# A written-out order of a two-stage kernel on one core, laid out anew for the landings of its first loads

## The chip, the core and the metric

The kernel runs on one core of a Trainium2 chip. A core has five engines that run side by side, each with its own queue of instructions which it works off in order: TensorE (PE, matmuls; PEld is its weight load), VectorE (DVE), ScalarE (ACT), GpSimd (POOL) and SyncE (SP, which here only issues DMAs). Matmuls write to PSUM, eight banks of 128 x 2 KB; ACT and DVE bring the results from there to the on-chip memory SBUF. The metric is the device time of one launch in microseconds, the median of several runs.

## What is computed

```python
# x (8, 8, 512, 64), state (8, 8, 32, 64): per batch b and head h
scores  = 0.125 * x @ state^T;   a  = softmax(scores over the 32 states)
scores2 = 0.125 * state @ x^T;   a2 = softmax(scores2 over the 512 tokens)
y = concat([a @ state, a2 @ x], axis=2)          # 8 x 8 x 544 x 64
h = y.reshape(8 * 544, 512) @ w_in               # w_in 512 x 2048
g = max(h, 0) + alpha * min(h, 0)                # alpha 2048
out = g @ w_out                                  # w_out 2048 x 512
```

## The kernel before

The kernel never forms `a @ state`: it multiplies the states with w_in first (m = state @ w_in, per batch and per quarter f of w_in's columns, on PE), and then h = a @ m. All operands of matmuls are 16 bit, sums are 32 bit. A batch has 512 tokens and 16 groups of 128 columns of h, called jc.

All work is cut into some fifty kinds of step (each a small function, lines 160 to 608), and the string ORDER (lines 17 to 102) writes out in which order the steps are issued: about 1060 words, each a step's name with its arguments, read at line 625. An engine's queue gets its instructions in that order. What has to wait for what (data, a buffer or a bank that is still read) is turned into semaphores by the framework. So the order decides three things: the place of each instruction in its engine's queue, the engine where a word carries a letter (a = ACT, v = DVE, p = POOL), and the PSUM bank where it carries a bank's number (0 to 5). The banks that are left make one double tile named `two`.

The words, by engine:

- POOL's queue. `lx0`: second half of the first x (L191, 256 KB as stored). `id`: the identity matrix. `lst`: the states of batches 1 to 7 (L207). `wi.f`: a quarter of w_in (L213). `wo.i`: a quarter of w_out (L219). `lx.b`: x of batch b (L162). All are DMA issues, and these loads turn 32 bit into 16. `ssh.p` subtracts the maximum (L360), `snorm.p` multiplies by one over the sum (L374), `tn` the same for the second softmax (L419).
- DMAs ahead of ORDER: the first half of the first x in two pieces (SP and ACT, L179), the states of batch 0 (ACT, L185), alpha (SP, L187).
- PE. `Z.k.n`: n matmuls of zeros into bank k (L232), which compute nothing. `stt`, `str.i.k`: transposed states of batch 0, of the others (L247). `xt.b.j.g.k`: four transposes of x of batch b into bank k (L299). `sc.b` (or `sc.0.0`, `sc.0.1` by halves): scores into `two` (L313). `m.b.f.k0.k1`: the two halves of m into two banks, or into `two` if no banks are given (L463). `f.b.jc.g.k`: half of one jc of h (L517). `F.b.jc.k`: one jc of h, two matmuls (L496). `S.b.q.j.k`: two of the 16 matmuls of an output row block q of batch b, with jc 2j and 2j+1 (L548). `rd.b.k`: the second softmax's reads (L438). `R`, `L`: the last blocks (L596, L568).
- ACT or DVE. `xc`: first x to 16 bit (L197). `sto`, `sro`: transposed states out of PSUM (L261, L281). `xo.b.j.g`: transposed x out (L304). `mo.b.f.e.g`: half g of m out (L485). `O`, `RO`, `LO`: outputs out, then a DMA on SP. `rdo`: the reads out (L449).
- DVE. `stc`: states to 16 bit (L253). `oma`: 1 - alpha (L269, L270). `sb`: scores as blocks (L348, L346). `smax`, `ssum`: maximum, sum and its reciprocal (L354, L370, L371). `wb`: the weights back, called aT (L382). `tm`, `tsum`: the second softmax's maximum and reciprocal (L394, L397, L415). `G.b.jc`: gt, the activation's result (L536).
- ACT. `sexp`, `te`: exponentials (L366, L405). `N.b.jc`: neg = max(-h, 0) (L528), which G reads.
- SP. `xd.b`, `tt.b`: transposes by DMA of x from batch 2 on, and of the second softmax's weights.

The first batch runs its first softmax by halves, so that f.0.jc.0 can start on the first half. m of several batches is made early, as soon as the first quarter of w_in is there. The slots of x hold four batches, those of m seven.

```python
    for token in (globals().get("TOKENS") or ORDER).split():
        name, *args = token.split(".")
        steps[name](*[int(a) if a.isdigit() else a for a in args])
```

Of the kernel before, what the change touches and what calls it, by code (L numbers as in the profile page):

```python
# [29 lines left out]
smax.1 N.0.11 S.0.2.3 m.0.3 G.0.8 F.0.10.5 tn.0.1 S.0.0.3 mo.0.3.a.0 G.0.9 N.0.10 G.0.11 ssh.p.1  # L30
S.0.3.0.3 mo.0.3.v.1 S.0.3.1 F.0.13.0 S.0.3.2 sexp.1 N.0.13 G.0.10 S.0.3.3 m.1.3 ssum.1 G.0.13
F.0.14.5 S.0.2.4 snorm.p.1 N.0.14 G.0.14 S.0.1.4 wb.1 tt.0 F.0.12.0 N.0.12 G.0.12 S.0.0.4 F.0.15.5
S.0.3.4 mo.1.3.a.1 N.0.15 tsum.1 tn.1.0 S.0.1.5 G.0.15 S.0.0.5 S.0.2.5 F.1.0.0 S.0.1.6 mo.1.3.a.0
F.1.2.5 N.1.0 lx.3 S.0.1.7 S.0.2.6 N.1.2 S.0.2.7 sc.2 O.0.2.a G.1.0 O.0.1.v G.1.2 S.0.0.6 S.0.0.7
F.1.5.0 F.1.1.1 F.1.6.5 tm.2 F.1.3.2 O.0.0.a xd.3 N.1.5 sb.2 S.0.3.5 N.1.1 F.1.7.4 G.1.5 S.0.3.6
N.1.6 N.1.3 S.0.3.7 F.1.4.0 G.1.1 S.1.2.0.1 te.2.1 G.1.3 N.1.7 N.1.4 O.0.3.a G.1.7 F.1.14.2 S.1.2.1
te.2.0 F.1.9.4 G.1.6 N.1.14 G.1.4 smax.2 rd.0.3 m.2.3 F.1.11.5 N.1.9 mo.2.3.a.1 G.1.9 F.1.8.0 tn.1.1
rdo.0.a G.1.14 mo.2.3.a.0 tt.1 ssh.p.2 N.1.8 S.1.2.2 lx.4 F.1.10.3 N.1.11 S.1.1.0.4 N.1.10 S.1.2.3
G.1.8 sexp.2 S.1.1.1 m.3.2 G.1.11 m.2.1.2.0 G.1.10 mo.3.2.a.0 S.1.1.2 mo.2.1.a.0 ssum.2 F.1.12.5
N.1.12 S.1.1.3 F.1.13.3 snorm.p.2 S.1.1.4 G.1.12 F.1.15.2 N.1.13 S.1.1.5 S.1.2.4 xd.4 S.1.2.5 N.1.15  # L40
mo.2.1.a.1 G.1.13 mo.3.2.a.1 G.1.15 S.1.1.6 m.2.2.5.3 mo.2.2.a.1 m.3.1.0.2 sc.3 wb.2 sb.3 S.1.2.6
mo.3.1.a.0 mo.2.2.a.0 S.1.2.7 S.1.0.0.3 mo.3.1.a.1 F.2.3.0 O.1.2.a S.1.0.1 N.2.3 smax.3 F.2.12.5
N.2.12 G.2.3 F.2.4.2 N.2.4 G.2.12 F.2.2.1 S.1.1.7 F.2.15.0 S.1.0.2 O.1.1.a tm.3 S.1.3.0.5 F.2.0.4
N.2.15 ssh.p.3 S.1.0.3 G.2.4 S.1.3.1 S.1.0.4 F.2.1.2 S.1.3.2 N.2.2 G.2.2 N.2.0 G.2.15 sexp.3 F.2.9.1
G.2.0 S.1.3.3 tsum.2 F.2.6.0 S.1.0.5 N.2.1 G.2.1 S.1.0.6 F.2.13.4 ssum.3 S.1.3.4 N.2.9 te.3.1
F.2.11.2 te.3.0 S.1.3.5 S.1.3.6 N.2.6 G.2.9 G.2.6 F.2.5.1 N.2.13 S.1.3.7 G.2.13 S.1.0.7 N.2.11
G.2.11 N.2.5 O.1.3.a tn.2.0 O.1.0.a F.2.7.0 rd.1.4 G.2.5 m.4.3.2.5 sc.4 m.3.3.1.3 tsum.3 rdo.1.a
mo.4.3.a.1 snorm.p.3 mo.3.3.a.1 wb.3 tn.2.1 N.2.7 mo.3.3.v.0 S.2.1.0.4 lx.5 mo.4.3.v.0 F.3.4.5 G.2.7
S.2.1.1 F.2.8.3 F.2.10.1 N.3.4 S.2.1.2 N.2.8 G.3.4 tt.2 F.3.6.2 N.2.10 G.2.8 G.2.10 F.3.8.0
S.2.0.0.5 N.3.8 F.3.7.3 N.3.6 S.2.1.3 S.2.1.4 N.3.7 F.3.9.1 S.2.0.1 N.3.9 S.2.1.5 tn.3.0 sb.4 tn.3.1  # L50
G.3.7 G.3.8 G.3.9 F.2.14.3 S.2.0.2 S.2.1.6 F.3.13.0 S.2.0.3 F.3.14.1 smax.4 xd.5 S.2.0.4 G.3.6
N.2.14 S.2.0.5 G.2.14 S.2.3.0.2 S.2.3.1 F.3.2.3 S.2.3.2 N.3.14 S.2.3.3 tm.4 N.3.13 S.2.0.6 ssh.p.4
G.3.14 S.2.3.4 S.2.0.7 F.3.1.1 G.3.13 F.3.3.0 sexp.4 te.4.1 ssum.4 te.4.0 N.3.2 S.2.1.7 S.2.3.5
G.3.2 S.2.3.6 tsum.4 S.2.3.7 tt.3 N.3.1 N.3.3 O.2.1.a O.2.0.a G.3.1 m.6.0 G.3.3 O.2.3.a mo.6.0.a.1
m.5.1.3.1 mo.6.0.v.0 snorm.p.4 m.4.2.4.0 rd.2.5 rd.3.2 mo.4.2.a.0 mo.5.1.a.0 rdo.3.a mo.4.2.v.1
rdo.2.v sc.5 m.4.1.4.0 m.5.0.5.3 mo.5.1.v.1 S.2.2.0.2 mo.4.1.a.0 F.3.10.1 tn.4.1 F.3.5.4 tn.4.0
mo.5.0.a.0 mo.4.1.a.1 N.3.10 tm.5 mo.5.0.a.1 S.2.2.1 F.3.11.5 S.2.2.2 F.3.0.0 S.2.2.3 wb.4 N.3.5
S.2.2.4 N.3.11 G.3.10 N.3.0 F.3.12.3 N.3.12 F.4.0.1 S.2.2.5 sb.5 G.3.5 S.2.2.6 lx.6 S.2.2.7 lx.7
te.5.0 F.4.9.4 N.4.0 te.5.1 G.3.11 G.3.12 G.3.0 tsum.5 O.2.2.a F.3.15.5 F.4.6.3 S.3.3.0.0 S.3.3.1
N.4.9 G.4.0 S.3.3.2 S.3.3.3 S.3.3.4 N.3.15 smax.5 S.3.3.5 F.4.5.2 G.3.15 G.4.9 F.4.3.1 tt.4 N.4.6  # L60
tn.5.0 tn.5.1 N.4.3 S.3.3.6 F.4.1.5 G.4.6 G.4.3 N.4.5 tt.5 S.3.0.0.4 G.4.5 S.3.0.1 F.4.4.3 N.4.4
S.3.0.2 ssh.v.5 N.4.1 F.4.2.1 S.3.3.7 S.3.0.3 S.3.0.4 O.3.3.a sexp.5 S.3.0.5 G.4.4 F.4.7.2 G.4.1
S.3.0.6 N.4.7 S.3.1.0.3 S.3.1.1 ssum.5 S.3.1.2 G.4.7 F.4.8.0 F.4.11.5 N.4.8 S.3.0.7 N.4.2 snorm.v.5
N.4.11 S.3.1.3 xd.6 S.3.1.4 S.3.1.5 O.3.0.a S.3.1.6 G.4.2 rd.4.2 G.4.8 rdo.4.a G.4.11 rd.5.1
m.5.3.4.0 rdo.5.a m.5.2.5.2 sc.6 wb.5 tm.6 mo.5.3.a.0 mo.5.2.a.1 S.3.2.0.1 S.3.2.1 F.4.10.4 N.4.10
S.3.2.2 S.3.2.3 S.4.1.0.2 S.3.1.7 S.4.1.1 S.3.2.4 mo.5.3.a.1 G.4.10 sb.6 smax.6 S.3.2.5 te.6.0
F.4.13.0 O.3.1.v N.4.13 F.5.15.4 N.5.15 G.4.13 S.4.1.2 S.3.2.6 S.3.2.7 te.6.1 F.4.12.3 F.4.14.0
ssh.p.6 m.6.3 G.5.15 mo.5.2.a.0 S.4.1.3 N.4.12 F.5.12.5 S.4.1.4 S.4.1.5 F.5.13.4 N.4.14 O.3.2.v
N.5.12 mo.6.3.v.0 G.4.12 S.4.0.0.1 N.5.13 G.5.12 G.4.14 sexp.6 F.5.3.3 S.4.0.1 F.5.0.5 G.5.13 tsum.6
N.5.3 mo.6.3.v.1 F.4.15.0 S.4.0.2 G.5.3 N.4.15 F.5.1.4 S.4.0.3 tn.6.0 F.5.2.3 S.4.1.6 S.4.0.4 G.4.15  # L70
N.5.0 S.4.1.7 S.4.0.5 xd.7 F.5.5.0 N.5.2 G.5.2 O.4.1.v F.5.10.3 S.4.0.6 N.5.1 G.5.0 N.5.5 N.5.10
G.5.1 m.6.1.2.5 m.7.0 S.4.0.7 S.4.3.0.4 mo.7.0.a.1 O.4.0.a G.5.5 S.4.3.1 mo.6.1.a.0 mo.7.0.v.0
S.4.3.2 G.5.10 F.5.8.0 mo.6.1.a.1 m.6.2.1.2 sc.7 m.7.2.3.5 ssum.6 S.4.3.3 sb.7 S.4.3.4 mo.6.2.a.1
mo.7.2.a.1 N.5.8 snorm.p.6 F.5.4.2 mo.7.2.a.0 S.4.2.0.5 S.4.3.5 S.4.2.1 S.4.2.2 S.4.2.3 smax.7
S.4.3.6 F.5.9.3 N.5.4 wb.6 S.4.3.7 G.5.4 S.4.2.4 mo.6.2.a.0 G.5.8 F.5.7.1 O.4.3.v N.5.9 G.5.9
S.5.2.0.2 ssh.p.7 tn.6.1 F.5.6.0 N.5.7 F.5.14.4 N.5.6 N.5.14 G.5.7 G.5.6 S.4.2.5 F.6.8.3 G.5.14
S.4.2.6 S.5.2.1 S.4.2.7 S.5.2.2 S.5.0.0.1 O.4.2.a sexp.7 S.5.0.1 tm.7 F.5.11.0 N.6.8 tt.6 F.6.3.4
ssum.7 F.6.0.5 G.6.8 S.5.2.3 N.5.11 S.5.0.2 N.6.3 G.5.11 S.5.0.3 G.6.3 te.7.0 snorm.v.7 S.5.0.4
N.6.0 S.5.2.4 te.7.1 F.6.15.3 S.5.1.0.0 S.5.1.1 tsum.7 F.6.1.4 S.5.1.2 N.6.1 G.6.0 G.6.1 N.6.15
S.5.1.3 S.5.1.4 wb.7 F.6.14.5 tn.7.0 S.5.0.5 S.5.1.5 F.6.7.4 G.6.15 S.5.2.5 S.5.2.6 N.6.14 F.6.10.3  # L80
S.5.1.6 S.5.0.6 G.6.14 S.5.2.7 N.6.7 tn.7.1 S.5.0.7 N.6.10 G.6.7 F.6.9.5 G.6.10 O.5.2.v F.6.5.4
N.6.5 O.5.0.v G.6.5 F.6.4.3 tt.7 F.6.6.2 S.5.3.0.1 S.5.3.1 N.6.9 N.6.6 S.5.1.7 S.5.3.2 F.6.2.4 G.6.6
S.5.3.3 S.5.3.4 O.5.1.a N.6.4 m.7.3.2.0 m.7.1 G.6.9 N.6.2 rd.6.5 G.6.4 rd.7.3 mo.7.3.a.1 rdo.7.a
S.5.3.5 F.7.0.0 S.5.3.6 rdo.6.v mo.7.3.v.0 mo.7.1.a.1 F.8.10.5 S.5.3.7 G.6.2 N.7.0 O.5.3.a G.7.0
F.6.13.3 F.6.12.2 N.8.10 S.6.0.0.4 G.8.10 N.6.12 F.6.11.0 S.6.0.1 N.6.13 F.8.3.1 G.6.12 S.6.0.2
N.6.11 F.7.3.5 G.6.11 mo.7.1.v.0 N.8.3 F.8.4.2 G.8.3 S.6.1.0.0 S.6.1.1 N.7.3 S.6.1.2 G.6.13 N.8.4
F.7.7.1 S.6.0.3 F.7.2.3 S.6.1.3 G.8.4 S.6.0.4 N.7.7 F.8.14.2 S.6.0.5 S.6.1.4 S.6.0.6 N.8.14 S.6.0.7
G.7.7 G.8.14 F.8.2.1 S.6.1.5 F.7.6.2 O.6.0.v G.7.3 F.8.9.4 S.6.1.6 S.6.2.0.5 N.8.2 N.7.2 S.6.2.1
# [569 lines left out]
```

## Time and profile before

| what | value |
|---|---|
| median of 3 runs | 218.68 us (218.29 to 218.93) |
| the profiled execution: its time, its span | 219.14 us, 217.3 us |
| PE busy, share of the span | 211.0 us, 97% |
| DVE, ACT, POOL busy | 169.2, 138.0, 64.8 us |
| moved by DMA | 23.39 MB, mean 108 GB/s; 196 GB/s from 1.1 to 25 us |
| issue and landing of the first loads | lx0 1.23 and 6.9; lst 2.74 and 8.3; wi.0 3.32 and 10.9; lx.1 4.07 and 13.6; wi.1 4.94 and 16.2; wo.0 5.83 and 18.7; wi.2 6.57 and 22.1; wo.1 12.35 and 23.9; wi.3 14.64 and 26.5 |

The span runs from the first instruction to the last; the rest of the profiled execution's time lies around it. A busy PE is not a PE at its peak: matmuls overlap, and a matmul of 512 columns is listed with 379 ns while the next one starts 216 ns after it. In a timeline a row is: start, busy time, engine, line, operation, what is written and read, shapes and count, and in brackets the idle time before it with what ended it.

### The profile page before, as it was taken

How to read it: one execution, taken by the hardware profiler on the slowest of the kernel's cores; microseconds unless marked ns; L12 is line 12 of the kernel's file. 1: busy time of each engine (PE TensorE's matmuls, PEld its weight loads, DVE VectorE, ACT ScalarE, POOL GpSimd, SP SyncE). 2: the span in 40 equal slices, each digit the busy share in tenths (PEclk: the TensorE clock that was granted, in tenths of full speed). 3: DMA queues.
4: the chain of work that ended last, by engine and by line, in shares of the span. 5: the costliest groups of instructions: out<-in, count | busy, mean ns of one | idle time of the engine just before them, and what ended most of it. 6: DMA issues, size and time to landing. Idle time of an engine off the chain costs nothing.

```text
span 217.3 us, 4301 instructions
## 1 busy us (share of the span) xinstructions
PE 211.0 (97%) x1692; PEld 104.1 (48%) x1692; DVE 169.2 (78%) x260; ACT 138.0 (63%) x271; POOL 64.8 (30%) x54
## 2 busy tenths in 40 slices
...
GB/s 148 180 205 207 206 202 160 63 250 168 98 162 3 168 109 113 148 129 163 103 142 0 134 62 98 0 108 41 0 195 51 0 48 51 48 38 10 51 97 145
DMA packets 39316, 23.39 MB, mean 108 GB/s; under 512 B 21872, under 2 KB 35328, under 8 KB 39296
## 3 DMA queue, kind: packets, MB, share of 16 engines
...
## 4 chain that ended last, share of the span: by engine, by line
PE 90%; DVE 6%; DMA 1%; ACT 1%; POOL 0%; issue 0%
PE o L548 49%; PE h L496 24%; PE m_ps L463 3%; PE h L505 3%; PE o L596 3%; DVE gt L536 2%; PE sr_ps L438 2%; PE o L568 2%; DMA st<-in_state_dram 1%; PE sc L313 1%; PE z L232 1%; PE xT_ps L299 1%; DVE aT L382 1%; DVE m L485 1%; DVE r L370 1%; DVE nb L394 1%
## 5 line engine op out<-in xcount | busy, mean ns | idle before, releaser
L548 PE MATMUL o<-w_out_sb,gt 128*128 128x512 f16 x496 | 126.4, 379 | 0.1
L528 ACT ACTIVATE neg<-h 128x512 f32<-128x512 f32 (+1 forms) x144 | 77.4, 580 | 45.2 <-PE h L496 31.4
L536 DVE SCALAR_TENSOR_TENSOR gt<-neg,oma_sb,h 128x512 f16<-128x512 f32 x128 | 89.7, 736 | 15.4 <-ACT neg L528 14.6
L548 PEld LDWEIGHTS <-gt 128*128 128x128 f16 x496 | 47.3, 98 | 54.9 <-issue 3.7
L496 PE MATMUL h<-aT,m 128*128 128x512 f16 x250 | 69.2, 379 | 0.3 <-DVE gt L536 0.3
L496 PEld LDWEIGHTS <-m 128*128 128x128 f16 x250 | 24.2, 98 | 29.7 <-issue 1.6
L419 POOL TENSOR_SCALAR e<-e,r 128x512 f16<-128x512 f16 x16 | 25.0, 1568 | 25.2 <-DVE r L415 20.6
L485 ACT CAST m<-m_ps 128x512 f16<-128x512 f32 x50 | 27.9, 603 | 3.7 <-PE m_ps L463 2.0
L360 POOL TENSOR_TENSOR ts<-ts,mx 128x1024 f32<-128x1024 f32 (+1 forms) x8 | 13.6, 1698 | 43.6 <-DVE mx L354 43.6
L586 ACT COPY osb<-o 128x512 f32<-128x512 f32 x22 | 12.8, 591 | 16.4 <-PE o L548 16.4
L374 POOL TENSOR_TENSOR an<-ts,r 128x1024 f16<-128x1024 f32 (+1 forms) x7 | 11.7, 1667 | 18.1 <-DVE r L371 18.0
L405 ACT ACTIVATE e<-sc,nb 128x512 f16<-128x512 f32 x16 | 11.1, 697 | 1.5 <-issue 1.5
L463 PE MATMUL m_ps<-w_in_sb,stT 64*32 64x512 f16 x256 | 11.7, 383 | 0.1
L536 DVE SCALAR_TENSOR_TENSOR gs<-neg,oma_sb,h 128x256 f16<-128x256 f32 x16 | 7.5, 476 | 5.1 <-ACT neg L528 5.1
L370 DVE TENSOR_REDUCE r<-ts 128x32 f32<-128x1024 f32 (+1 forms) x9 | 9.8, 1093 | 1.3 <-ACT ts L366 1.3
L485 DVE CAST m<-m_ps 128x512 f16<-128x512 f32 x14 | 9.3, 684 | 1.6 <-ACT m L485 1.4
L382 DVE STREAM_TRANSPOSE aT<-an 128x1024 f16<-128x1024 f16 (+1 forms) x9 | 10.0, 1114 | 0.5 <-POOL an L374 0.4
L354 DVE TENSOR_REDUCE mx<-ts 128x32 f32<-128x1024 f32 (+1 forms) x9 | 9.9, 1096 | 0.1
L394 DVE TENSOR_REDUCE nb<-sc 128x2 f32<-128x1024 f32 x8 | 9.7, 1212 | 0.1
L232 PE MATMUL z<-zero 128*128 128x128 f16 x76 | 7.6, 263 | 1.9 <-DVE zero L226 1.1
L606 DVE COPY osr<-o 128x512 f32<-128x512 f32 x1 | 0.7, 692 | 11.3 <-PE o L596 11.3
L505 PE MATMUL h<-XS,w_in_sb 128*128 128x256 f16 x64 | 9.4, 273 | 0.0
...
## 6 DMA issues: line engine op xcount, KB each, us to landing
...
w_in_sb<-in_moe_w_in_dram POOLq DMA_DIRECT2D x4, 512.0 KB, 11.6
...
```

The costliest lines, as they stand in the source:

```text
L360: engine(e).tensor_tensor(ts, ts, over_blocks(cols(live["mx", b], j, S // N)), ALU.subtract)
L370: nc.vector.tensor_reduce(r1, blocks(cols(live["ts", b], j, S)), AX.X, ALU.add)
L382: nc.vector.transpose(cols(live["aT", b], j, S), cols(live["an", b], j, S))
L419: nc.gpsimd.tensor_scalar_mul(e2, e2, live["r2", b][:, g : g + 1])
L463: nc.tensor.matmul(t[N * k : N * (k + 1), :], st_head(b, h)[64 * r : 64 * r + 64, :], w_in_sb[64 * r : 64 * r + 64, c, 512 * f : 512 * (f ...
L485: copier(e)(m_tile(b)[:, f, g, :], live["mp", b, f][g])
L496: nc.tensor.matmul(h.rearrange("p (r j s) -> p r j s", r=2, j=2), ms[b][:, f, g, 128 * j : 128 * (j + 1)], weights(b, g), start=(g == 0), ...
L505: nc.tensor.matmul(h, w_in_sb[:, c, 128 * jc : 128 * (jc + 1)], XS[:, c].rearrange("p q n b -> p (q n b)"), start=(c == 0), stop=(c == n_c ...
L528: nc.scalar.activation(neg, h, RELU, bias=0.0, scale=-1.0)
L536: nc.vector.scalar_tensor_tensor(gt, negs.pop((b, jc)), oma_sb[:, jc : jc + 1], h, ALU.mult, ALU.add)
L548: nc.tensor.matmul(outs[b, q], gts[b, jc][:, 128 * q : 128 * (q + 1)], w_out_sb[:, jc, :], start=(jc == 0), stop=(jc == n_jc - 1),)
L586: copier(e)(osb, t)
```

## The change

Only the string ORDER changes, all of it; no function does. The same steps are issued in another order, with other banks, and some on another engine. The part that lies at the start:

```diff
-lx0 id lst stc xc.1.v xc.0.a oma wi.0 lx.1 Z.1.20 stt.0 Z.2.9 xt.0.1.0.1 xt.0.0.0.2 xo.0.1.0.v
-xo.0.0.0.v sto.a Z.0.7 sc.0.0 xt.0.1.1.3 xt.0.0.1.4 str.0.5 sb.0.0 xo.0.0.1.v xo.0.1.1.a Z.1.4
-sc.0.1 smax.0.0 str.1.0 sro.0.a wi.1 sb.0.1 wo.0 smax.0.1 wi.2 ssh.p.0.0 sro.1.a sexp.0.0 Z.1.3 sc.0
-m.0.0.1.2 ssh.p.0.1 mo.0.0.a.0 Z.5.5 m.1.0.3.4 m.2.0.5.0 tm.0 mo.2.0.a.0 ssum.0.0 sexp.0.1
-mo.1.0.a.0 mo.2.0.a.1 wo.1 Z.1.12 m.3.0.1.5 Z.3.7 xt.1.1.0.3 snorm.p.0.0 mo.1.0.v.1 te.0.1
-mo.3.0.a.1 ssum.0.1 wb.0.0 xt.1.0.0.4 xo.1.1.0.v te.0.0 xo.1.0.0.v wi.3 xt.1.1.1.0 snorm.p.0.1 Z.3.9
-f.0.0.0.5 mo.0.0.a.1 xo.1.1.1.v xt.1.0.1.3 wo.2 f.0.2.0.4 tsum.0 m.1.1 wb.0.1 mo.3.0.a.0 xo.1.0.1.v
-m.0.1.0.2 mo.1.1.v.0 tn.0.0 mo.0.1.v.0 f.0.2.1 f.0.0.1 mo.1.1.a.1 mo.0.1.a.1 f.0.1.0.1 f.0.1.1
-F.0.3.3 m.4.0 N.0.0 N.0.1 F.0.5.2 N.0.2 F.0.4.0 G.0.0 G.0.1 N.0.3 G.0.2 F.0.7.5 N.0.5 N.0.4 G.0.3
-S.0.1.0.1 mo.4.0.a.0 S.0.0.0.4 mo.4.0.a.1 G.0.4 S.0.0.1 S.0.1.1 lx.2 N.0.7 m.0.2.3.0 sc.1 G.0.5
-mo.0.2.a.0 S.0.2.0.2 wo.3 G.0.7 m.1.2.5.3 mo.0.2.a.1 mo.1.2.a.0 S.0.2.1 sb.1 F.0.6.0 xd.2 mo.1.2.a.1
...
+lx0 id stc xc.1.v xc.0.a Z.1.26 stt.0 Z.2.9 xt.0.1.0.1 xt.0.0.0.2 xo.0.1.0.a oma lst sto.v
+xo.0.0.0.v Z.4.7 sc.0.0 xt.0.1.1.3 sb.0.0 wi.0 xt.0.0.1.4 str.0.5 lx.1 xo.0.0.1.a xo.0.1.1.v
+smax.0.0 sc.0.1 sb.0.1 wi.1 sro.0.a ssh.p.0.0 str.1.0 sro.1.a sexp.0.0 smax.0.1 Z.1.3 sc.0 Z.5.3
+m.0.0.1.2 m.1.0.3.4 ssh.p.0.1 mo.1.0.a.1 m.3.0.5.0 Z.4.28 xt.1.0.0.4 wo.0 wi.2 mo.0.0.a.1 tm.0
+mo.3.0.v.0 sexp.0.1 ssum.0.0 mo.0.0.a.0 mo.1.0.a.0 ssum.0.1 mo.3.0.v.1 snorm.p.0.0 xt.1.1.1.5
+m.2.0.2.1 xt.1.1.0.3 te.0.1 wb.0.0 mo.2.0.a.1 te.0.0 xt.1.0.1.0 Z.1.3 f.0.0.0.1 mo.2.0.a.0
+xo.1.1.0.a xo.1.0.0.v f.0.1.0.4 m.0.1 snorm.p.0.1 xo.1.0.1.v wb.0.1 wo.1 m.1.1.0.2 f.0.0.1
+mo.0.1.a.1 xo.1.1.1.v N.0.0 mo.0.1.v.0 f.0.1.1 F.0.3.3 mo.1.1.v.0 G.0.0 wi.3 f.0.2.0.5 N.0.1 f.0.2.1
+wo.2 F.0.4.0 tsum.0 G.0.1 m.4.0 lx.2 tn.0.0 mo.1.1.a.1 F.0.7.1 F.0.5.2 N.0.2 S.0.1.0.4 N.0.3 G.0.2
+mo.4.0.a.0 N.0.5 N.0.7 N.0.4 wo.3 G.0.3 S.0.0.0.5 G.0.5 S.0.0.1 mo.4.0.a.1 S.0.1.1 m.0.2.3.2 G.0.7
+sc.1 G.0.4 F.0.6.1 mo.0.2.a.1 m.1.2.2.0 mo.0.2.a.0 S.0.2.0.3 sb.1 mo.1.2.a.0 tm.1 S.0.2.1 mo.1.2.a.1
...
```

In the rest the sequence of PE's steps differs up to batch 5; from the last steps of batch 6 on it is the same, with other banks. Counted over the whole string: zeros 79 instead of 76; out copies 25 on ACT and 6 on DVE instead of 22 and 9; m copies 48 and 16 instead of 50 and 14; `rdo` 5 and 3 instead of 6 and 2; `xo` 3 and 5 instead of 1 and 7; `ssh.v.5`, `snorm.v.5` and `snorm.v.7` become `.p`.

More of the change, by code (lines that the diff above doesn't have):

```diff
@@ L30 @@
[L30 to L88, printed above, removed]
@@ new lines @@
+S.0.1.7 tsum.1 tn.1.1 S.0.2.6 G.1.0 S.0.2.7 O.0.1.a sc.2 m.2.1.2.4 G.1.2 S.0.0.6 O.0.2.a mo.2.1.a.1
+F.1.1.1 sb.2 S.0.0.7 S.0.3.5 mo.2.1.a.0 tm.2 F.1.5.3 F.1.4.4 F.1.3.2 N.1.1 G.1.1 O.0.0.a N.1.5 G.1.5
+lx.3 N.1.4 N.1.3 S.0.3.6 F.1.9.5 N.1.9 F.1.12.1 F.1.14.3 G.1.4 G.1.3 N.1.12 F.1.6.4 S.0.3.7 F.1.7.2
+G.1.9 G.1.12 N.1.6 S.1.1.0.5 S.1.1.1 tn.1.0 te.2.0 O.0.3.a smax.2 F.1.8.1 S.1.2.0.0 N.1.7 G.1.6
+S.1.2.1 te.2.1 N.1.14 N.1.8 G.1.7 G.1.14 S.1.1.2 F.1.11.4 N.1.11 ssh.p.2 S.1.2.2 G.1.8 S.1.1.3
+S.1.2.3 sexp.2 m.3.1.2.3 m.2.3 mo.2.3.a.1 G.1.11 S.1.1.4 mo.2.3.v.0 ssum.2 mo.3.1.a.0 F.1.10.1
```

81 lines of the change are left out of this document (67 added, 14 removed).

## The prediction, made before the changed kernel ran

> **What bounds the kernel now.** I read the page first, then busy time by stretches, the chain of waits in order of time, the timeline of each engine up to 30 us, and the landing time of each load. The first two say that TensorE (PE) is the bound and where it is not.
>
> ```profile
> span 217.3 us, 4301 instructions
> ...
> PE 211.0 (97%) x1692; PEld 104.1 (48%) x1692; DVE 169.2 (78%) x260; ACT 138.0 (63%) x271; POOL 64.8 (30%) x54
> ```
>
> The second view, busy time by stretches (length; then busy us of PE, PEld, DVE, ACT, POOL, the clock, DMA share, GB/s):
>
> ```profile
> 25.06:214.40 189.34, 189.26 (x1408) 90.57 (x1408) 150.88 (x221) 120.47 (x239) 47.36 (x30) 1.00 0.47 97
> ```
>
> From 25.06 us to its last matmul PE lacks 0.08 us of 189.34. So whatever is moved after 25 us can gain nothing; it can only add a stall. A gain must come from what happens before, where the chain of waits runs over other engines:
>
> ```profile
> 14.90 0.58 DVE aT L382
> 15.48 1.05 POOL an L374
> ...
> 16.56 0.71 DVE aT L382
> 17.27 0.31 DVE xT L304
> 17.58 0.69 DVE m L485
> ...
> 18.29 1.07 ACT m L485 x2
> 19.36 0.51 ACT neg L528
> ...
> 19.90 4.71 DVE gt L536 x7
> ```
>
> The reader is to see the order DVE, then ACT, then DVE: two casts of m on ACT (18.29 to 19.36) lie on the path, and the seven gt start only at 19.90. PE's useful stream follows them: S.0.1.0 starts at 21.36, after the second gt. The waits tell why ACT was late:
>
> ```profile
> ACT m L485 <- DVE m L485: 1.1, 1, 1.1
> DVE m L485 <- ACT m L485: 1.4, 2, 1.2
> ```
>
> ACT stood 1.1 us for a DVE cast although it reads another half: m.1.1 lies in the double bank `two`, and where the halves of one such tile go to two engines the second waits for the first (the other row is the same in the other direction, at 89.63). Halves in two single banks do not wait: mo.1.0.a.0 at 13.36 and mo.1.0.v.1 at 13.40 ran side by side.
>
> **The change part by part.** It is an order alone. Up to S.0.1.0 both orders have the same steps of use on PE (m.0.0, m.1.0, m.2.0, m.3.0, m.0.1, m.1.1, m.4.0, sixteen transposes per batch as before, f.0.0 to f.0.2, F.0.3, .4, .5, .7), and after it the same rest, so the time is decided by when that point comes.
>
> *"Other states behind the first x".* On POOL's queue lx0, id, lst, wi.0, lx.1, wi.1 stand in this order before and after. The states land at 8.3 (issued 2.74, 5.6 to landing) either way. Price: nothing.
>
> *First evacuations.* sto moves from ACT to DVE (128x256; between 0.17, the smallest DVE row, and 0.43, the 128x512 copy; I take 0.3), xo.0.1.0 from DVE to ACT (0.59 by the one ACT copy, hidden: ACT was idle 2.9 us there). DVE, busy with alpha until 6.42, then does sto and xo.0.0.0 until 6.42+0.3+0.41 = 7.13 instead of two copies until 7.17. Then xo.0.1.1 goes to DVE straight after the first block transpose and xo.0.0.1 to ACT: ready at 8.61 (7.57+1.04), done 9.25. Z.1.4 is gone, so sc.0.1 starts at 9.27 instead of 9.46 and every DVE step from there, token max (11.20) included, about 0.2 earlier: 10.98. If the ACT copy is late by more than 0.2 this is lost, at no further cost, for the next paragraph has its own bound.
>
> *ACT's queue to the first neg.* It starts with the states' copies, which need the landing at 8.3 and str.0.5, so at 9.25 in both:
>
> ```profile
> 9.25 2.22 ACT L281 COPY stT<-st_ps 128x896 f16<-128x896 f16 x2 [0.45 <-PE st_ps L247]
> 11.34 0.62 ACT L366 ACTIVATE ts<-ts 128x512 f32<-128x512 f32 x1
> ...
> 16.12 1.11 ACT L485 CAST m<-m_ps 128x512 f16<-128x512 f32 x2
> 18.29 1.07 ACT L485 CAST m<-m_ps 128x512 f16<-128x512 f32 x2 [1.06 <-DVE m L485]
> 19.25 3.07 ACT L528 ACTIVATE neg<-h 128x512 f32<-128x512 f32 x6
> ```
>
> Up to 16.12 both queues hold the same counts (two exponentials, five casts, two token exponentials); only which m differs. After that the old one had two casts, the wait, two casts, and neg at 19.25. The new one has mo.2.0.a.0, xo.1.1.0.a, mo.0.1.a.1: 16.12 + 0.55 + 0.53 + 0.55 = 17.75, with no wait, for m.0.1 needs the token exponentials gone from `two` (16.2) and w_in's second part (4.94 + 11.3 = 16.2). f.0.0 is ready at 17.6, so N.0.0 starts at 17.75 to 17.8: 1.5 earlier.
>
> *DVE's queue to the first gt.* From 10.98, start to start in the old rows: token max 1.32, one cast 0.57, two sums with reciprocals 0.88 each, a second cast 0.58, aT 0.6, two xT copies 0.65, aT 0.63, a copy 0.38: 17.47. Then mo.0.1.v.0 waits for mo.0.1.a.1 (same `two` rule) until 17.8, takes 0.6, mo.1.1.v.0 0.6, and G.0.0 starts at **19.0** instead of 19.90. The old queue had one cast less but 1.04 idle. tsum.0 now stands behind G.0.0: +0.15. So G.0.1 starts at 19.82 instead of 20.57, and the rest follows at 0.671 each (4.70 for seven): G.0.2 20.49, .3 21.16, .5 21.83, .7 22.50, .4 23.17, each 0.735 long.
>
> *PE behind it.* Single banks are written again only when evacuated. F.0.4 waits for mo.1.1.v.0 (19.1), m.4.0 19.6, F.0.7 19.93, F.0.5 20.36, S.0.1.0 20.8 (old 21.36), S.0.0.0 21.28 (bank 5 behind G.0.2), S.0.0.1 21.95 (G.0.3), S.0.1.1 22.38, m.0.2 22.9, sc.1 23.2 (behind mo.4.0.a.1, which now stands after three neg on ACT, done 23.15), F.0.6 23.45, m.1.2 23.97 (banks behind mo.0.2.a.1 and G.0.4), S.0.2.0 24.35, S.0.2.1 until 25.25. The old trace had the same set done when F.0.6, starting at 25.43, was: 25.43+0.43 = 25.86. Difference **-0.6**, between -0.3 (each of the two chains 0.15 later) and -1.5 (neg's own gain, were DVE free).
>
> *Loads.* The issues of wo.0 and wi.2 move behind both subtracts on POOL: 12.2 and 13.0 instead of 5.83 and 6.57. Queued behind them on POOL are only the two multiplications, of which the first waits for DVE until 14.0 anyway. Cover: the queue is still moving wi.1, landed at 16.2, and wo.1, issued at 12.35 before, was late for nobody. Earliest landing by the least loaded row of this size (6.9 from issue): wo.0 19.1, wi.2 one transfer (2.6) later, 21.7; old 18.7 and 22.1. First users: S.0.1.0 at 20.8, m.0.2 at 22.9. Price if the cover is gone: see rival 3.
>
> *Zeros.* 79 instead of 76. Z.1.26 runs 1.10 to 3.8 (26 at 102 ns) under the wait for the states at 4.18; Z.4.28 starts when mo.1.0.a.1 is done (12.5) and takes 28 x 58 ns = 1.6, until 14.1, under the second x, landed at 13.6. Price 0 while the array runs at its full rate, which the weight loads show as 102 ns each and then 58:
>
> ```profile
> 1.10 2.05 PEld L232 LDWEIGHTS <-zero 128*128 128x128 f16 x20 [1.10 <-DVE zero L226]
> ...
> 9.13 0.23 PEld L232 LDWEIGHTS <-zero 128*128 128x128 f16 x4
> ```
>
> A rule that speaks against this stands in the Trainium skill, TensorE: Matmul & The Clock Gate, Part 1: the clock is let go after one busy window of some 3.4 us which runs freely, so the moment differs from run to run. This trace agrees in so far as the rate changed once, between 7.0 and 9.1. By that rule fillers counted for the fast rate sometimes run at the slow one; that is rival 4.
>
> *After 25 us.* Other banks and engines for the same steps: three out copies move from DVE to ACT (0.59 instead of 0.69), two m casts and one XS cast to DVE, one subtract and two normalisations of batches 5 and 7 from DVE (1.22) to POOL (1.91). All stand tens of PE instructions ahead of their users: F of batch 5 comes 27 us of PE work behind sc.5, and PE, idle for 0.08 us in 189, hides them. By the order, the nearest reuse of a bank is 0.86 us of PE work behind its evacuation's start, before 0.78. Price 0; if one cast were late, some 0.5 once. The last batch and the tail have the same order.
>
> Sum: 0 + 0 - 0.6 + 0 = -0.6. The profiled execution took 219.14 (span 217.34 and 1.80 around it), 0.46 over the median of 218.68. So the span goes to 216.7 and the median to **218.1**.
>
> **Rivals.** (1) *The gain is larger*: the DVE casts do not hold gt back and the 1.5 of neg comes through in good part. For it: PE's stalls between 20 and 25 us sum to 1.2 and are all on gt or casts. Against: DVE has no idle left. About -1.1: 217.6.
> (2) *Nothing arrives*: the change names landings that do not move, and DVE is busy 1.9 to 2.0 of each 2 us from 10 to 18; if its rows stretch to the sum of full durations (the 0.05 to 0.15 of overlap at each step lost over ten steps), G.0.0 is at 19.75 and tsum.0 eats the rest: 218.6.
> (3) *Slower, the late w_in*: wi.2, issued 6.4 later, lands as the old wo.1 did from its issue: 13.0 + 11.6 = 24.6. m.0.2 stands in PE's queue ahead of sc.1 and all S.0.2; it would wait 1.7, less the 0.6: 219.7. It decides from a landing after 23.5. Against: wo.1 had three transfers ahead of it, wi.2 has two.
> (4) *A slow array under Z.4.28*: 28 x 44 ns = 1.2 later on m.2.0, whose cast is on ACT's chain at 14.98: the gt would start at 20.0, +0.3 with tsum.0: 219.0.
>
> **How the numbers follow.** Forecast 0.55, larger 0.15, nothing 0.18, late w_in 0.08, slow array 0.04. No change means within 0.3% (0.66 us), about what a measurement of this kernel can tell: three runs spread over 0.64. The forecast's -0.6 lies beside that bound: half of its 0.55 counts as faster, with rival 1 that makes 0.28 + 0.15 = 0.43; same is 0.27 of the forecast, 0.16 of rival 2 and 0.02 of rival 4, together 0.45; slower is rival 3 and 0.02 each of rivals 2 and 4, together 0.12. Range 217.3 to 219.3: down to rival 1 and the spread, up past rivals 2 and 4, short of 3.
>
> **What would show it.** Right: first neg near 17.8 without a wait on DVE, first gt near 19.0, S.0.1.0 near 20.8, PE full from 25 us on, lst landing still at 8.3. Wrong: the first gt after 19.6, m.0.2 released by a DMA, zeros at 12.5 with 102 ns each, or PE idle on a bank after 25 us.

## The result and the profile after

The change made the kernel slower: 220.47 us (median of 6 runs, 219.54 to 220.75) against 218.88 us (6 runs, 218.29 to 218.93), a ratio of 1.0070 with an interval of 1.0047 to 1.0093. The prediction had 218.1 us and a range of 217.3 to 219.3. The profiled execution of after took 220.75 us, that of before 219.14. The page of after begins:

```profile
span 218.9 us, 4303 instructions
...
PE 210.2 (96%) x1695; PEld 102.6 (47%) x1695; DVE 165.3 (75%) x256; ACT 139.1 (64%) x272; POOL 70.3 (32%) x57
```

The span is 1.6 us longer, and PE is busy 0.8 us less. Busy time by stretches says where PE now waits. First before (start:end, length, then busy us of PE, PEld, DVE, ACT, POOL, the clock, DMA share, GB/s), then after:

```profile
25.80:45.00 19.20, 19.20 (x117) 8.16 (x115) 17.72 (x26) 14.20 (x29) 7.89 (x5) 1.00 1.03 147
45.00:75.00 30.00, 30.00 (x274) 13.59 (x273) 28.70 (x42) 26.59 (x53) 14.66 (x10) 1.00 0.69 141
...
130.00:140.00 10.00, 10.00 (x89) 4.20 (x88) 9.66 (x13) 6.72 (x13) 3.96 (x3) 1.00 0.14 53
```

```profile
25.80:45.00 19.20, 18.94 (x120) 7.90 (x119) 17.12 (x25) 13.91 (x28) 7.88 (x5) 1.00 1.04 158
45.00:75.00 30.00, 29.64 (x264) 13.21 (x262) 28.46 (x41) 26.17 (x53) 10.98 (x7) 1.00 0.68 119
...
130.00:140.00 10.00, 9.65 (x145) 4.55 (x143) 8.96 (x16) 6.39 (x13) 3.46 (x2) 1.00 0.15 54
```

Before, PE had no idle time in these three stretches; after, it lacks 0.26, 0.36 and 0.35 us. These numbers understate the loss, since a busy PE is not a PE at its peak: where matmuls stand singly their tails no longer overlap. So I also read the list of PE's instructions for its *lag*: the time at which after has done a given amount of useful work (each matmul weighed by its start-to-start distance in a full stream), less the time at which before had done it. The lag is -0.06 us at 26 us, +0.58 at 38, +0.93 at 58, +1.30 at 64 and +1.63 from 140 us to the end, and 219.14 + 1.63 = 220.77 is the time of the profiled execution to 0.02. So two things went otherwise than forecast: the start brought nothing in this execution (-0.06 instead of -0.6), and 1.69 us were lost after 26 us, where the forecast had 0.

The waits of after name the second (engine and line that waited, what it waited for: us in total, times, longest):

```profile
DVE m L485 <- ACT m L485: 5.8, 5, 2.2
...
ACT m L485 <- DVE m L485: 1.1, 1, 1.1
```

Before, casts of m on DVE waited twice for casts of m on ACT, 1.4 us in all; now five times and 5.8 us, one of them in the start. Each of these is a tile of m in the double bank `two` whose halves go to two engines. The chain of waits of after runs through one of them at 30 us (start, us, what) and through another at 53:

```profile
29.86 0.61 DVE m L485
...
30.98 0.60 ACT neg L528
31.58 0.95 ACT ts L366
...
32.56 1.23 DVE r L370
...
34.31 1.92 POOL an L374
...
36.26 1.25 DVE aT L382
37.51 0.64 DVE gt L536
...
38.19 0.59 PE h L496 x2
```

The reader is to see that no user of m stands in this chain. The cast on DVE at 29.86 holds up the cast on ACT, and what is late is what is queued behind that cast on ACT: a neg and the exponential of batch 1's softmax. From there the delay goes over the sum, the normalisation on POOL, aT and a gt to PE at 38.19, 8 us after its cause; PE's lag grows between 34 and 38 us.

### The profile page after: what moved, and what is told of

It reads as the page before. It is cut to its first block, busy times and chain, and to the rows that moved or that the text cites. A ratio compares the mean times of both kernels' runs of the same rounds, so it can differ in the third digit from the quotient of the medians.

```text
span 218.9 us, 4303 instructions
## 1 busy us (share of the span) xinstructions
PE 210.2 (96%) x1695; PEld 102.6 (47%) x1695; DVE 165.3 (75%) x256; ACT 139.1 (64%) x272; POOL 70.3 (32%) x57
## 4 chain that ended last, share of the span: by engine, by line
PE 75%; DVE 12%; DMA 5%; POOL 3%; ACT 3%; issue 1%; POOLq 0%
PE o L548 42%; PE h L496 20%; DMA xg<-in_x_dram 5%; DVE gt L536 4%; PE h L505 3%; PE o L596 3%; PE m_ps L463 2%; DVE m L485 2%; POOL an L374 2%; PE o L568 2%; PE sr_ps L438 2%; ACT m L485 1%; DVE aT L382 1%; DVE r L370 1%; DVE mx L354 1%; DVE ts L346 1%
## 5 line engine op out<-in xcount | busy, mean ns | idle before, releaser
L548 PE MATMUL o<-w_out_sb,gt 128*128 128x512 f16 x496 | 125.0, 379 | 0.1
L360 POOL TENSOR_TENSOR ts<-ts,mx 128x1024 f32<-128x1024 f32 (+1 forms) x9 | 15.5, 1718 | 43.7 <-DVE mx L354 43.7
L485 ACT CAST m<-m_ps 128x512 f16<-128x512 f32 x48 | 26.7, 601 | 3.7 <-PE m_ps L463 2.3
L374 POOL TENSOR_TENSOR an<-ts,r 128x1024 f16<-128x1024 f32 (+1 forms) x9 | 15.4, 1719 | 41.2 <-DVE r L371 22.1
L586 ACT COPY osb<-o 128x512 f32<-128x512 f32 x25 | 14.7, 591 | 16.5 <-PE o L548 16.5
L485 DVE CAST m<-m_ps 128x512 f16<-128x512 f32 x16 | 10.6, 684 | 5.8 <-ACT m L485 5.8
L463 PE MATMUL m_ps<-w_in_sb,stT 64*32 64x512 f16 x256 | 11.2, 383 | 0.2 <-DMA w_in_sb<-in_moe_w_in_dram 0.2
L382 DVE STREAM_TRANSPOSE aT<-an 128x1024 f16<-128x1024 f16 (+1 forms) x9 | 10.1, 1117 | 1.1 <-POOL an L374 1.1
L346 DVE STREAM_TRANSPOSE ts<-sc 128x1024 f32<-128x1024 f32 x7 | 8.7, 1241 | 0.8 <-PE sc L313 0.8
## 6 DMA issues: line engine op xcount, KB each, us to landing
w_in_sb<-in_moe_w_in_dram POOLq DMA_DIRECT2D x4, 512.0 KB, 10.1
```

The costliest lines, as they stand in the source:

```text
L360: engine(e).tensor_tensor(ts, ts, over_blocks(cols(live["mx", b], j, S // N)), ALU.subtract)
L374: engine(e).tensor_tensor(blocks(cols(live["an", b], j, S)), blocks(cols(live["ts", b], j, S)), over_blocks(cols(live["r1", b], j, S // N) ...
L382: nc.vector.transpose(cols(live["aT", b], j, S), cols(live["an", b], j, S))
L463: nc.tensor.matmul(t[N * k : N * (k + 1), :], st_head(b, h)[64 * r : 64 * r + 64, :], w_in_sb[64 * r : 64 * r + 64, c, 512 * f : 512 * (f ...
L485: copier(e)(m_tile(b)[:, f, g, :], live["mp", b, f][g])
L548: nc.tensor.matmul(outs[b, q], gts[b, jc][:, 128 * q : 128 * (q + 1)], w_out_sb[:, jc, :], start=(jc == 0), stop=(jc == n_jc - 1),)
```

## The experiments

The experiments change only words of the order. All times are medians; the ratio is to the kernel before, measured on the same chip in the same job. Before had 218.88 beside after and 218.69 beside e1 to e4, so a difference between the medians of after and of one of these carries some 0.2 us of that; the ratios are free of it.

**One cast in m.0.3 (e1).** In after, ACT and DVE have the same queues as here; only the word that is read first, and so the half that the other has to wait for, differs.

```diff
-mo.0.3.v.1 S.0.2.3 mo.0.3.a.0
+mo.0.3.a.0 S.0.2.3 mo.0.3.v.1
```

> The changed kernel with the two halves of m.0.3 taken in the other order of words: the ACT half ahead of the DVE half. The queue of every engine is the same; only which half waits for which is turned round. Theory A (halves of one double tile on two engines wait for each other, and the one that waits holds up what stands behind it): the 1.09 us wait of ACT before that cast goes, the exponential of batch 1 starts near 30.9 instead of 31.47, aT of batch 1 near 35.7 instead of 36.26, PE's gaps between 32 and 38 us shrink from 0.7 to under 0.2, and the median falls by 0.4 to 0.6 from 220.47, to about 219.95. Theory B (the losses after 25 us come from the loads that are issued later and from the steps moved to POOL): no change, 220.2 to 220.7, and the gaps stay.

Measured: 219.86 (219.27 to 220.04, 8 runs), 1.0049 [1.0033, 1.0064], 0.6 less than after (0.5 by the ratios). Timelines of ACT, after first, then e1:

```profile
30.50 0.59 ACT L485 CAST m<-m_ps 128x512 f16<-128x512 f32 x1 [1.09 <-DVE m L485]
...
31.47 1.06 ACT L366 ACTIVATE ts<-ts 128x1024 f32<-128x1024 f32 x1
```

```profile
28.58 0.59 ACT L485 CAST m<-m_ps 128x512 f16<-128x512 f32 x1
...
29.77 1.06 ACT L366 ACTIVATE ts<-ts 128x1024 f32<-128x1024 f32 x1
```

The wait of 1.09 on ACT is gone, and with it the loss between 26 and 40 us: the lag goes from -0.88 at 26 us to -0.86 at 40, in after from -0.06 to +0.58. From 26 us to the end it grows by 1.08 instead of 1.69. By the traces m.0.3 is worth 0.6.

**One engine in m.2.3 (e2), the cast ahead of the reads in m.7.0 (e3), and all three together (e4).**

```diff
-mo.2.3.v.0
+mo.2.3.a.0
...
-rdo.5.a mo.7.0.a.1
+mo.7.0.a.1 rdo.5.a
```

> The changed kernel with the second half of m.2.3 on ACT as well, instead of DVE. Theory A: DVE's 0.89 us wait at 53.2 goes, the sum of batch 2 starts at 52.4 instead of 53.8, the stall of 0.46 between the two reads near 55.6 and the 0.37 near 64 go, median down by 0.5 to 0.8, to about 219.8. Theory B: ACT has one more cast (0.59) and nothing is gained: 220.3 to 220.8.

> The changed kernel with ACT's half of m.7.0 moved ahead of the copy of the reads of batch 5, so that DVE's half needn't wait. Theory A: DVE's 0.96 us wait near 134 goes, scores of batch 7 start without a wait, gaps of 0.6 near 135 to 136 us go, median down by 0.4 to 0.7, to about 219.9. Theory B: no change, 220.2 to 220.7.

> The changed kernel with all three edits. Theory A: the gains add, 1.4 to 1.9, so 218.6 to 219.1: level with the kernel before, as its start gained nothing. Theory B: 220.2 to 220.8.

Measured: e2 219.73 (219.56 to 220.44, 6 runs), 1.0053 [1.0034, 1.0072]; e3 219.36 (219.14 to 220.09, 12 runs), 1.0036 [1.0023, 1.0048]; e4 218.93 (218.20 to 219.47, 12 runs), 1.0013 [0.9999, 1.0027]. In after, m.7.0 looks like this on DVE and PE:

```profile
134.81 1.88 DVE L485 CAST m<-m_ps 128x512 f16<-128x512 f32 x3 [0.96 <-ACT m L485]
...
135.55 0.41 PE L313 MATMUL sc<-xT,stT 64*32 64x256 f16 x16 [0.16 <-DVE m L485]
136.15 0.59 PE L496 MATMUL h<-aT,m 128*128 128x512 f16 x2 [0.18 <-DVE m L485]
```

ACT does a reads copy at 133.90, after a wait on PE, and only then its half of m.7.0 at 134.09; DVE idles 0.96 for that, the other half and two more casts come late, and PE stands twice. With the cast ahead of the reads copy (e3) ACT does it at 132.32, and DVE does not wait:

```profile
133.15 1.30 DVE L485 CAST m<-m_ps 128x512 f16<-128x512 f32 x2
```

In e3 the lag stays at +0.54 from 130 to 140 us where after's goes from +1.04 to +1.63. The growth of the lag from 26 us to the end is 1.11 in e3, 1.51 in e2 and 0.28 in e4. So by the profiles m.0.3 costs 0.61, m.7.0 0.58 and m.2.3 0.18, or 1.41 together; by the medians the three cost 220.47 - 218.93 = 1.54, by the ratios 1.25 (1.0070 less 1.0013). That is the loss after 26 us but for some 0.3 us, and none of the three edits touches a load or a step on POOL, which theory B blames. e4 still has three such waits on DVE, 3.6 us in all with one of 2.2; nothing that PE needs soon is queued behind these, and they cost nothing that the lag shows.

e2's median lies where its theory had it, but the mechanism does only in part. DVE no longer waits at 53.2, yet the stall between the two reads stays (0.23 of idle time before 55.68, in after 0.29 before 56.03), because the fourth cast of m on ACT now makes a neg late, for which DVE waits:

```profile
54.88 2.22 DVE L536 SCALAR_TENSOR_TENSOR gt<-neg,oma_sb,h 128x512 f16<-128x512 f32 x3 [1.29 <-ACT neg L528]
```

The trace gives the edit 0.18 of the 0.74 by which the median fell (0.4 by the ratios). That the median met the theory is luck. e3's fell by 1.1 (0.7 by the ratios) where its theory had 0.4 to 0.7 and its trace has 0.58.

**The same arrangement put into the kernel before (f4).** If the cause is the pair of halves and not something else in the new order, the old order must become slow by it. DVE's half of m.0.3 comes first here; the queue of each engine stays as it was.

```diff
-mo.0.3.a.0 G.0.9 N.0.10 G.0.11 ssh.p.1 S.0.3.0.3 mo.0.3.v.1
+G.0.9 G.0.11 mo.0.3.v.1 mo.0.3.a.0 N.0.10 ssh.p.1 S.0.3.0.3
```

> The kernel BEFORE with the words of the two halves of m.0.3 in the other order, the DVE half first; every engine's queue is the same as before. Theory A: ACT waits for DVE's cast at 30.7 and starts its own near 31.4 instead of 29.89, the exponential of batch 1 comes 1.5 later, aT of batch 1 holds DVE up, and PE gets gaps between 33 and 39 us: median up by 0.7 to 1.5, 219.4 to 220.2. Theory B: no change, 218.4 to 218.9.

Measured: 220.42 (220.32 to 220.47, 6 runs), 1.0075 [1.0049, 1.0101]. The direction is as the theory has it and the size more than the 0.7 to 1.5 that it gave: 1.7 over the before of its job (218.73). Timelines of ACT, before first, then f4:

```profile
29.89 0.59 ACT L485 CAST m<-m_ps 128x512 f16<-128x512 f32 x1
...
30.89 1.05 ACT L366 ACTIVATE ts<-ts 128x1024 f32<-128x1024 f32 x1
```

```profile
31.20 0.58 ACT L485 CAST m<-m_ps 128x512 f16<-128x512 f32 x1 [1.71 <-DVE m L485]
...
32.17 1.06 ACT L366 ACTIVATE ts<-ts 128x1024 f32<-128x1024 f32 x1
```

ACT waits 1.71 instead of after's 1.09, the exponential starts at 32.17 (30.89 in before), aT at 36.96 (35.68 in before), and the lag goes from -0.25 at 26 us to +1.28 at 40 and stays. One pair of casts of 0.6 us, with the same work in the same queues, makes the old kernel as slow as the whole change did.

**What is left after 26 us (h1, h2).** Both stand on f3 (below), which has e4's rest. In e4 the second softmax's reads wait at 54 us for a gt, whose neg stands on ACT behind four casts of m. h1 gives the last of these to DVE, which idles there; m.3.1 lies in two single banks. h2 also moves a token maximum on DVE behind two gt.

```diff
-mo.3.1.a.1
+mo.3.1.v.1
...
-tm.3 S.1.0.2 N.2.15 ssh.p.3 G.2.6 G.2.3
+S.1.0.2 N.2.15 ssh.p.3 G.2.6 G.2.3 tm.3
```

> On top of f3 (218.07): mo.3.1.a.1 goes to DVE, which idles 1.29 us at 52 us while ACT works off four casts ahead of N.1.10. m.3.1 lies in two single banks. Theory (what is left of the loss after 25 us comes from casts of m that stand ahead of a neg on ACT): N.1.10 starts 0.5 earlier, the stall of 0.40 in the second softmax's reads at 54 to 56 us is gone, the lag from 26 us to the end falls by 0.3 to 0.4, median 217.7. Rival (only halves of the double tile matter, and two single banks on two engines cost nothing and bring nothing): 218.0 to 218.1, the stall stays.

> On top of h1: the token maximum of batch 3 on DVE (2.1 us) goes behind G.2.6 and G.2.3. Theory: the stall of 0.22 at 63 to 65 us goes, 0.2 under h1, 217.5. Rival: the next exponential of the tokens is then late and the same time is lost there: same as h1 within 0.1.

Measured: h1 217.62 (217.21 to 218.75, 12 runs), 0.9941 [0.9916, 0.9966]; h2 218.40 (218.09 to 219.08, 12 runs), 0.9984 [0.9966, 1.0002]. In e4, ACT and PE read as follows at this place:

```profile
50.83 2.05 ACT L485 CAST m<-m_ps 128x512 f16<-128x512 f32 x4 [0.34 <-PE m_ps L463]
```

```profile
53.31 0.68 PE L438 MATMUL sr_ps<-e2T,xg 128*64 128x32 f16 x32
54.22 0.68 PE L438 MATMUL sr_ps<-e2T,xg 128*64 128x32 f16 x32 [0.23 <-DVE gt L536]
```

In h1 they read:

```profile
50.59 1.56 ACT L485 CAST m<-m_ps 128x512 f16<-128x512 f32 x3 [0.34 <-PE m_ps L463]
```

```profile
53.07 1.19 PE L438 MATMUL sr_ps<-e2T,xg 128*64 128x32 f16 x64
```

ACT is free for the neg at 52.03 instead of 52.75 (0.24 of this is the earlier start of h1's execution), and the two reads have become one run of 64 matmuls without a break. From 26 us to the end the lag falls by 0.04 instead of growing by 0.28, so h1's theory holds. One stall of 0.3 us, at 62 to 64 us, is left in h1; about as much is won at other places. DVE's cast of m.3.1 ran at 51.80 while ACT's third cast, its other half, ran from about 51.6: halves in two single banks do not wait. Both halves go to the same tile of m in SBUF, as those in `two` do, so it is the shared tile in PSUM that makes one wait for the other. The Trainium skill, PSUM — Partial Sum Buffer, Specifications (TRN2), says that ScalarE and VectorE read PSUM in parallel as long as they are not on the same bank. h1's two casts agree with it. The halves of `two` lie in two banks as well, so by that rule the wait would be one of the semaphores that go by the tile, and not of the chip; no run here took it away with the tile kept.

h2 lost what it was to win and more, 0.78 against h1 in the same job. Its PE:

```profile
63.24 1.02 PE L548 MATMUL o<-w_out_sb,gt 128*128 128x512 f16 x4 [0.86 <-DVE gt L536]
```

In h1 the maximum runs at 58.59, in time in which DVE in h2 idles 1.19 us for a neg. Put behind the two gt, it runs from 61.12, the five gt that follow start only at 62.45, and PE waits 0.86 us. Neither the theory (0.2 gained) nor the rival (the same time) has this size.

**The start: late weights? (f2).** In after wo.0 and wi.2 are issued at 11.70 and later. f2 is e4 with both ahead of the first subtract on POOL.

```diff
-ssh.p.0.0
+wo.0 wi.2 ssh.p.0.0
...
-wo.0 wi.2 mo.0.0.a.1
+mo.0.0.a.1
```

> The kernel with all three edits, with wo.0 and wi.2 issued ahead of the two subtracts on POOL, as in the kernel before. Theory E (the second x lands later because of the later issues behind it): it lands at 13.6 or earlier in the profile, and the median falls by 0.3 to 0.5, to 218.4 to 218.6. Theory F (its landing scatters by itself): no change, 218.7 to 219.1.

Measured: 219.06 (218.25 to 220.18, 12 runs), 1.0005 [0.9982, 1.0028]; e4 had 1.0013. No difference that can be told, within the 0.5 us to either side that the interval leaves. In f2's profile the second x landed 10.1 us after its issue, as in e2, where the weights are issued late; so nothing speaks for the theory that the late issue delays it.

**The start: m.2.0 behind the second x (f1), and the order of two casts (f3).** In after, PE stands at 14.5 us for the second x, with m.2.0 queued behind its transposes. f1 is e4 with m.2.0 ahead of both of them, f3 is f1 with the two casts ahead of the first gt turned on DVE.

```diff
 f1
-xt.1.0.0.4
...
-xt.1.1.1.5 m.2.0.2.1
+m.2.0.2.1 xt.1.0.0.4 xt.1.1.1.5
 f3, on top
-mo.0.1.v.0 f.0.1.1 F.0.3.3 mo.1.1.v.0
+mo.1.1.v.0 f.0.1.1 F.0.3.3 mo.0.1.v.0
```

> The kernel with all three edits (218.93), and m.2.0 ahead of the transposes of the second x on PE. Theory C (the start gains nothing because those transposes wait for the second x, and m.2.0, whose cast is on ACT's chain to the first neg, stands behind them): the cast of m.2.0 starts near 15.0 whatever the landing, the first gt at 18.4 to 19.0, and the median falls by 0.2 to 0.5, to about 218.6. Theory D (the start is bound by DVE's own rows): no change, 218.8 to 219.1.

> The kernel with all three edits, m.2.0 ahead as in the first of this call, and on DVE mo.1.1.v.0 ahead of mo.0.1.v.0, so that the 0.88 us wait of DVE for the other half of m.0.1 is filled. Theory C with the rule of the double tile: first gt at 18.0 to 18.5, median 0.5 to 1.0 below 218.93, 217.9 to 218.4, which would be under the kernel before. Theory D: the same as the first of this call within 0.2.

Measured: f1 218.63 (217.89 to 220.18, 12 runs), 1.0001 [0.9979, 1.0024]; f3 218.07 (217.85 to 219.91, 13 runs), 0.9971 [0.9954, 0.9988]. f1 alone can't be told from e4; f3 is faster than the kernel before. What it turns is once more a half of `two`: mo.0.1.v.0, which waits for ACT, no longer stands ahead of mo.1.1.v.0. The two differ by 0.6 in their medians, but their intervals overlap.

The profiles show more than the medians. In g1 (below), which has f3's start, the second x landed 10.2 us after its issue and the first gt still stood at 18.13; with after's order of these steps landings of 10.1 us gave 19.22 (e2) and 19.20 (f2). f1 and h1, with m.2.0 ahead as well, had 18.12 and 18.09 at landings of 8.8 and 9.2. So with m.2.0 ahead the first gt no longer follows the second x. f3's own profile does not show it: its execution is the longest of the 13 (219.91), the second half of the first x landed at 8.2 instead of the 5.9 to 7.2 of the other profiles, and the first gt came at 20.05.

**The start with the rest exchanged (g1, g2).** Starts, up to mo.1.1.a.1, in front of the old order's remaining steps: g1 with f3's start, g2 with after's own.

```diff
 g1, g2: words of f3 or of after up to and with mo.1.1.a.1, then
 the words of before that are not among them, in before's order
```

> The start of the last kernel but with its two repairs (m.2.0 ahead of the second x, DVE's casts turned), up to mo.1.1.a.1, and from there the order of the kernel before. The theories so far: the repaired start is worth 0.6 to 0.9 and the old rest has no stall, so 217.7 to 218.0, at or under 218.07, with PE idle for under 0.2 us after 26 us. If the old rest leans on the old start (other moments at which buffers and x come free): 218.1 to 218.6 with gaps of PE between 26 and 45 us.

> The changed kernel's own start up to mo.1.1.a.1, then the order of the kernel before. If the prediction's 0.6 for the start was right and the rest alone lost it: 218.0 to 218.2. If the start is worth 0.1 or less in the median, because it follows the landing of the second x, which scatters: 218.5 to 218.8.

Measured: g1 218.28 (217.76 to 218.95, 12 runs), 0.9983 [0.9971, 0.9996]; g2 219.20 (218.34 to 220.59, 12 runs), 1.0024 [1.0004, 1.0044]. g1 lies 0.3 above its first theory; its second has the number but not the reason, for it asked for gaps of PE between 26 and 45 us, and the lag shows none. g2 lies 0.4 above the higher of its two theories. The joint is one reason: in both, some 0.45 us more are lost between the first gt and 26 us than in after itself. So these two do not measure the start alone. What they do show is the rest: the lag keeps its value of 26 us to the end within 0.01 in both, so the old rest loses nothing behind either start.

**The old start with two casts turned, and with more zeros (g3, g4).** Each is the kernel before with one edit.

```diff
 g3
-mo.1.1.a.1 mo.0.1.a.1
+mo.0.1.a.1 mo.1.1.a.1
 g4
-Z.1.20
+Z.1.26
```

> The kernel BEFORE with ACT's two casts mo.0.1.a.1 and mo.1.1.a.1 in the other order, so that ACT casts the half from a single bank while DVE is at the other half of the double tile. Theory A: ACT's wait of 1.06 near 18 shrinks to under 0.6, first neg 0.3 to 0.5 earlier, first gt near 19.4, median 0.2 to 0.5 lower: 218.2 to 218.5. If DVE's own rows set the first gt: 218.6 to 218.8.

> The kernel BEFORE with 26 zeros instead of 20 ahead of the states. The zeros alone are worth nothing by the prediction (price 0): 218.5 to 218.9. The array may change to its full rate some 3.4 us earlier in the profile (zeros after the states at 56 instead of 98 to 113 ns), as it did in most profiles of the new start; if the rate bounded the start, the median would fall by 0.2 to 0.4.

Measured: g3 218.29 (217.85 to 218.66, 12 runs), 0.9988 [0.9977, 1.0000], within the 218.2 to 218.5 expected; g4 218.78 (218.50 to 219.07, 12 runs), 1.0006 [0.9996, 1.0017], no difference. g3 lets ACT do first the half that waits for nothing, and DVE's first gt waits 0.56 us (at 18.72) instead of the 1.04 of the start that it changes.

So the pair that the prediction found in the old start could be had there with one exchange, for 0.24 us by the medians of its job (218.53), though the interval just reaches no change.

**The kernel before, profiled again (h3).** No edit; the question is where its profiled execution had lost the 0.46 us by which it lay over the median.

> The kernel before, unchanged, for a second profile of its start. Theory (the profiled execution of before lay 0.46 over its median wholly in its start): its time less 219.14 equals its first gt less 19.90 within 0.15, and from 26 us on the lag stays constant; median 218.5 to 218.8. Rival (scatter lies after 25 us too): the two differences disagree by more than 0.3.

Measured: 218.73 (218.16 to 219.08, 12 runs), 0.9993 [0.9976, 1.0011]; this profiled execution took 218.62. Its first gt:

```profile
19.39 2.72 DVE L536 SCALAR_TENSOR_TENSOR gt<-neg,oma_sb,h 128x512 f16<-128x512 f32 x4 [1.04 <-ACT neg L528]
```

It starts at 19.39 instead of 19.90, 0.51 earlier; the execution is 0.52 shorter; and the lag is -0.50 at every point from 18 us to the end. The theory holds: what differs between these two executions of the kernel before is the start alone. Here the first states were cast at 3.38 (3.69 in the profile of before) and the first x at 4.82 (5.12).

## Why the prediction was wrong, step by step

**After 25 us: "Price 0; if one cast were late, some 0.5 once."** This is the step that failed, and most of the error (the median came 2.4 over the forecast): 1.69 us in the profiled execution, of which 1.41 go with the three pairs that e4 changes. The rule itself stood in the prediction, read off the waits of before ("where the halves of one such tile go to two engines the second waits for the first"), but it was applied to the start alone. For the rest I listed steps that change their bank or engine, counted how far ahead of their users on PE they stand (27 us for batch 5), and took that as cover. Two of the three pairs are not even in that list. m.0.3 and m.7.0 have the same halves on the same two engines in both orders; what changed is the place of a word, DVE's half of m.0.3 ahead of ACT's, and ACT's half of m.7.0 behind a reads copy. Only m.2.3 is a cast moved to DVE. And the cover, where it is real, does not help: late were the neg, exponentials and other casts queued behind the waiting half on the same engine, and the sum, normalisation, aT and gt behind these. f4 shows it with nothing else changed. "Some 0.5 once" was the right size of one such case (0.61 and 0.58), but there were three, and f4's one cost 1.5 in its profile.

**The sum's base: "So the span goes to 216.7 and the median to 218.1."** The -0.6 was worked out against the profiled execution of before and then taken off the median as well. h3 shows that the 0.46 between the two lay wholly in the very start that was replaced, so most of the gain was already in the median. With the new start's first gt at 19.0 the lag at 26 us is -0.57 (e3, next point); h3's old start has -0.50. Taking from the medians of after, e1 to e4 and f2 the growth of their lag after 26 us gives 218.78, 218.78, 218.22, 218.25, 218.65 and 218.78, 218.6 on average, beside 218.5 to 218.9 for the kernel before: the start is worth about 0.1.

**The start's working was right under its condition.** G.0.0 was to start at 19.0; in after it started at 19.53. The reason is a landing: the second x, issued at 4.07, landed 10.4 us later (at 14.5), not 9.5 as in before. Timeline of PE, ACT and DVE in after:

```profile
14.54 0.62 PE L299 MATMUL xT_ps<-ident,xg 128*128 128x128 f16 x8 [0.62 <-DMA xg<-in_x_dram]
...
15.57 0.59 ACT L485 CAST m<-m_ps 128x512 f16<-128x512 f32 x1 [0.77 <-PE m_ps L463]
...
19.53 0.74 DVE L536 SCALAR_TENSOR_TENSOR gt<-neg,oma_sb,h 128x512 f16<-128x512 f32 x1
```

m.2.0 stands behind these transposes, its cast on ACT is at 15.57 instead of the 14.98 forecast, and everything to the gt moves by that. In e3, where the second x came after 9.5 us, as in before, the same lines read:

```profile
15.06 0.59 ACT L485 CAST m<-m_ps 128x512 f16<-128x512 f32 x1 [0.19 <-PE m_ps L463]
...
19.02 0.74 DVE L536 SCALAR_TENSOR_TENSOR gt<-neg,oma_sb,h 128x512 f16<-128x512 f32 x1
```

That is the forecast (15.0 and 19.0), and the lag at 26 us is -0.57, the -0.6 of the sum. In the six profiles with after's start, landings of 10.4, 9.2, 10.1, 9.5, 8.4 and 10.1 us from issue gave first gt at 19.53, 18.71, 19.22, 19.02, 18.39 and 19.20 (after, e1 to e4, f2). The old start did not follow it: 9.5, 10.1 and 10.4 gave 19.90, 19.65 and 19.84 (before, f4, g4), and 10.1 gave 19.39 in h3. So the new order exchanged a start bound by casts for one bound by a load whose landing varies; the prediction had this landing in its list as a constant, 13.6, and no rival for it.

**What held.** The states landed at 8.3 from the same issue. From the first gt to 26 us the working held to 0.1: it turned a first gt 0.9 earlier into 0.6 at 26 us, so 0.3 were to be lost on the way, and 0.31 were (a first gt 0.37 earlier left a lag of -0.06). The late issues of wo.0 and wi.2 cost nothing that shows: m.0.2 started at 23.22, released by no DMA, and f2 found nothing; rival 3, the late w_in, did not occur. (By its own terms, 218.68 + 1.7 - 0.6, it is 219.8 and not 219.7.) Z.4.28 took 1.6 to 1.7 us, as forecast, so rival 4 did not occur either. Rival 2, that nothing arrives, is what the medians of the start say, for another reason than the one that it gave: DVE's rows did not stretch. No rival stood for a cast of the double tile after 25 us, though the prediction's own list of what would refute it had "PE idle on a bank after 25 us".

What stays open: in the profiles the new start's first gt, less the 0.31 lost behind it, is 0.37 ahead of the old one's on average (six profiles against before, f4, g4 and h3); in the medians it is 0.1. Landings scatter by 2 us, and no run held them fixed.
